# Attention with inserted projection work: the second half of v in 6 and 5 steps a tile, and the insertions as a fixed list

## The chip, the cores and the metric

The kernel runs on one core of one Trainium2 chip. The metric is the device time of one execution in microseconds (us), as the median of several runs.

## The reference

Two layers, each an attention block followed by a Fourier mixing block, on x of 2048 rows (S) and 640 columns (D), in float32.

```python
def _A_ref(x, wqkv, wo):             # H = 32 heads, Dh = 20
    qkv = (x @ wqkv).reshape(B, S, 3, H, Dh).transpose(2, 0, 3, 1, 4)
    q, k, v = qkv[0], qkv[1], qkv[2]
    scores = einsum("bhqd,bhkd->bhqk", q, k) * Dh ** -0.5
    o = einsum("bhqk,bhkd->bhqd", softmax(scores), v)
    return o.transpose(0, 2, 1, 3).reshape(B, S, D) @ wo

x = A_x                              # twice:
x = x + _A_ref(_layernorm(x), A_wqkv, A_wo)
x = x + _B_ref(_layernorm(x), ...)   # Fourier mixing by DFT matrices
```

## The kernel before

**Phases of a layer.** A prologue normalizes and transposes x, makes the first chunk of q and of k (128 columns each, that is six heads and a bit) and the first half of v for all 16 row tiles. Then comes the attention sweep, which is most of a layer's time. The rest of the projection (the other chunks of q and k, and the second half of v) is inserted into the sweep. After it come the output projection and the Fourier block.

**The sweep.** `Attention.steps` is a list of 512 steps (g, qb, kc): 8 groups g of 4 heads, 4 query blocks qb of 512 rows, 16 key tiles kc of 128 rows. Below, step n is the place in this list; 16 steps are one q block, 64 one group. A step has
- two calls of `scores` (two heads each): two matmuls into one of three `psc` tiles in PSUM (L613), then one exponential on ScalarE over 128x1024 numbers (L616);
- one call of `values`: four matmuls, one a head, that add e x v to the accumulator `acc` (L624; the profile has each of them as two records). There is one `acc` bank. At kc = 15 `finish` follows: VectorE transposes `acc` out (L631), divides by the sum, transposes back, splits the result, and POOL writes it to DRAM. `values` of kc = 0 of the next block can begin when L631 has read the bank.

**The inserted work.** `Qkv.work` is a generator. Each `next` on it emits some matmuls: a block of a chunk of q or k (15 matmuls `pqk` of 128x512 for one of four column blocks tb, in pieces of 8 and 7 or three times 5), or a tile of the second half of v (15 matmuls `pv` of 128x320 in one piece, then a copy on VectorE, L314). Both use the one PSUM bank `fill`. After a block `keep` splits it on VectorE and POOL writes it to DRAM; some steps later a function `after` adds a small matmul `pn` and its maximum, and after a chunk's last block splits the next chunk's weights and fetches those after them on SP's queue. The chunks come in the order of `order` (i = 0 to 7); in the code before, the 16 tiles of v stand between chunks 3 and 4.

**The order of instructions** is written out by hand (the tile framework runs in manual schedule). A string fixes it for some steps: `s` is one call of `scores` (half a step), `v` one of `values`, `f` the next piece of inserted work, `n` the function owed after a block. The two strings of the sweep (`plan`):

```python
if n % 4 == 1 and n + (4 if whole else 8) < s.THIN and (whole or s.blocks % 2 == 0):
    return "sssfsssvvssvv" if whole else "sssfsssvvssvvsssfssvvsssnvv"
```

The first (4 steps) inserts a tile of v, the second (8 steps) one block of q or k. They begin at step 1: 16 blocks (steps 1 to 128), 16 tiles of v (129 to 192), 5 blocks (193 to 232). I call the second the dense string. From step 236 (`THIN`) on, the thin part, steps alternate "ss v", and `fill` inserts one piece of five matmuls where n % 16 is 2, 7 or 12; the step with a piece has no `v`, and two steps later there are two. A block thus takes 16 steps, and 11 blocks last until step 412. From step 448 on other strings (`tail`) insert the output projection.

In the thin part and in all strings, work for `compare` (checks of the DFT matrices, which run on VectorE and load by POOL's queue) goes along at a pace set by n alone.

`begin` makes sure, with `need`, that what a group reads has been made. Before, group 4 (from step 256) needs the whole second half of v ("v") at step 240. `Attention.values` reads 32 columns of a tile of v at 21 columns a head, so the last head of group 3 also reads columns that belong to the second half; their products are not used.

Of the kernel before, what the change touches and what calls it, by code (L numbers as in the profile page):

```python
# [6 lines left out]
F32R = mybir.dt.float32r  # L7
# [35 lines left out]
def mha_fnet_kernel(ctx, tc, x_in, wqk, wv, wo, seq, hid, nat_seq, nat_hid, out):  # L43
# [102 lines left out]
    class Qkv:  # L146
# [199 lines left out]
        def prologue(s, vals, xt, fill, att):  # L346
# [30 lines left out]
            def ones(t):  # L377
                s.v[t] = vals(f"v{t}", [H * VW + 12], F32, "v")
                G.memset(s.v[t][:, :H * VW].rearrange("p (a c) -> p a c", c=VW)[:, :, DH:], 1.0)
                G.memset(s.v[t][:, H * VW:], 1.0)  # L380

            for t in range(NT - ND):
                ones(t)
# [89 lines left out]
            s.made |= {0, ND}  # L473


        def work(s):

            order = [ND + 1, 1, ND + 2, 2, ND + 3, 3, ND + 4, 4]
            w = {0: s.w1}

            def chunk(i):
                c = order[i]
                for tb in range(NB):
                    p = bank("fill", [128, 512], "pqk")
                    for more in pieces([s.product(p, w[i], tb, dc) for dc in range(ND)], 8 if (i, tb) < (5, 1) else 5):
                        if more:
                            yield True
                    sq = s.keep(p, c, tb, True, s.fill)

                    def after():  # L490
                        s.norms(lambda *a: bank("fill", *a), c, tb, sq)
                        s.made.add((c, tb))
                        if tb == NB - 1:
                            s.made.add(c)
                            if i + 1 < len(order):
                                w[i + 1] = s.weights(s.fill("w", [2, ND, 128], F32R, "wqk"), order[i + 1], True)
                            if i + 2 < len(order):
                                s.fetch(order[i + 2])
                    yield after

            for i in range(4):
                yield from chunk(i)
            for t in range(NT):
                p = bank("fill", [128, HD], "pv")
                for more in pieces([s.value(p, t, dc) for dc in range(ND)], 15):
                    if more:
                        yield True
                s.own(p, t, 1, True)
                yield None
            s.made.add("v")  # L510
            for i in range(4, 8):
                yield from chunk(i)

            s.silent = True
            r = s.bounds()
            ok = const.tile([128, 1], F32, name="ok", bufs=2)
            V.tensor_scalar(ok[:H], r[:H, 2:3], (GUARD / SCALE) ** 2, None, op0=OP.is_le)

            def after():
                p = bank("fill", [1, 1], "pok")  # L520
                PE.matmul(p, ok[:H], one[:H], start=True, stop=True)
                V.tensor_scalar(s.flag, p, float(H), None, op0=OP.is_equal)
            yield after
# [23 lines left out]


    class Attention:
        THIN = 236  # L550

        def __init__(s, qkv, L):
            s.a = qkv
            s.k, s.q, s.e = {}, {}, {}
# [93 lines left out]
        def sweep(s, shift, begin, fill=lambda n: None, plan=None, block=None, compare=lambda n: None):  # L648
            done = calm = n = 0

            def opened(n):
                g, qb, kc = s.steps[n]
                begin(n, g, qb, kc)
                last = qb == NB - 1
                if kc == (7 if last else 10 if g in LATE else 4) and not (last and g == H // 4 - 1):
                    s.qload(*((g, qb + 1) if not last else (g + 1, 0)), shift)
                if last and g + 1 < H // 4:
                    for f, j in {1: [(0, 0)], 9: [(0, 1)], 11: [(1, 0)]}.get(kc, []):
                        s.kload(g + 1, f, j)
                if qb == 0 and kc == 0 and g:  # L660
                    s.kload(g, 1, 1)

            while n < len(s.steps):
                opened(n)
                order = plan and plan(n)
                if order:

                    while done < n - 1:
                        s.values(done)
                        done += 1  # L670
                    t = 2 * n
                    for c in order:
                        if c == "s":
                            m, j = divmod(t, 2)
                            if not j and m > n:
                                opened(m)
                            s.scores(m, j)
                            if j:
                                compare(m)
                            t += 1  # L680
                        elif c == "v":
                            s.values(done)
                            done += 1
                        else:
                            (block if c == "f" else fill)(t // 2)
                    n = t // 2
                    continue
                s.scores(n, 0)
                s.scores(n, 1)
                more, owed = fill(n) and n >= 2 and n + 1 < len(s.steps), n - 1 - done  # L690
                compare(n)
                n += 1
                if plan and n <= s.THIN:
                    count = owed + 1
                elif more and owed < 3:
                    calm = n + 1
                    continue
                else:
                    count = min(owed, 1)
                    if owed > 1 and (done + 1) % NT and n > calm:  # L700
                        calm = n + 1
                        count = 2
                for _ in range(count):
                    s.values(done)
                    done += 1
            for n in range(done, len(s.steps)):
                s.values(n)

        def run(s, done, project, check):
# [8 lines left out]
                           8: "sssfssvssvsvssvssvssvssvv"}[steps]  # L718
                n += steps

            def due(n):
                return s.blocks < 58 or s.blocks >= 91 or (n - 1) % NT in (2, 7, 12)

            def block(n):
                if not s.work:
                    project.parts.pop(0)()
                    return
                try:
                    f = next(work)
                    s.blocks += 1  # L730
                    s.more = f is True
                    s.after = (n + (2 if n < s.THIN else 4), f) if f and not s.more else None
                    s.rest = s.after[0] + 2 if s.after else n
                except StopIteration:
                    s.work = False
                    tasks.extend(done())

            def fill(n):
                if s.after:
                    if n >= s.after[0]:  # L740
                        f, s.after = s.after[1], None
                        f()
                elif s.work and n >= max(s.rest, s.THIN) and due(n + 1):
                    block(n)
                    s.rest = max(s.rest, n + 2)
                    return s.work and not s.a.silent

            def plan(n):
                if n in tail:
                    return tail[n]  # L750
                if s.blocks >= 58 or s.after:
                    return
                whole = 32 <= s.blocks < 48
                if n % 4 == 1 and n + (4 if whole else 8) < s.THIN and (whole or s.blocks % 2 == 0):
                    return "sssfsssvvssvv" if whole else "sssfsssvvssvvsssfssvvsssnvv"

            def compare(n):

# [18 lines left out]

            def begin(n, g, qb, kc):


                if qb == NB - 1 and g + 1 < H // 4:
                    when, to = 0, g + 1
                    c0, c1 = to * 80 // 128, ((to + 1) * 80 - 1) // 128
                    keys = [c0, (c1, 0) if to in LATE else c1, ND + c0, ND + c1] + (["v"] if to >= 4 else [])
                else:
                    when, to, keys = 5, g, [(((g + 1) * 80 - 1) // 128, qb + 1)]
                if to != g or g in LATE and qb < NB - 1:
                    if kc == when:
                        need(n, *keys)
                        s.shift = s.a.bound(to, s.room)  # L790
                    if kc - when in (0, 3, 5):
                        next(s.shift)

                if tasks and n % 2 == 0 and n >= 16 and n % 64 < 54:
                    tasks.pop(0)()
                for f in project.early.get(n, []):
                    f()
# [955 lines left out]
```

## Time and profile before

| | |
|---|---|
| median of 3 runs | 2439.93 us (2438.36, 2442.01, 2439.93) |
| profiled execution, its own time | 2440.27 us |
| its span, first to last instruction | 2438.5 us |
| TensorE's granted clock | 0.998 of full |
| busy: matmuls (PE), weight loads (PEld) | 2408.8, 1154.0 us |
| busy: ScalarE (ACT), VectorE (DVE), POOL | 2098.3, 1011.4, 555.9 us |
| exponentials (L616) | 2048, busy 1917.2 us |
| matmuls of values (L624), of scores (L613) | busy 1030.6 and 743.7 us |
| inserted and prologue matmuls `pqk`, `pv` (L106) | busy 320.5 and 151.7 us |

The sweep of layer 0 lasts from about 82 to 1094 us of the span, that of layer 1 from 1293 to 2307 us. A row of a group names line, engine, operation, output<-inputs, shapes, count, then busy time, mean ns of one, and the idle time of the engine just before it with what ended it. Rows of a timeline give start, length, engine, line, operation; rows of like instructions that follow each other are merged. Ends of matmuls are modelled, so their starts are the better measure.

### The profile page before, as it was taken

Reading aid. Unit: us, or ns where it says so; the run is one execution under the profiler, and the core shown is the slowest. Engines: PE = TensorE matmul, PEld = TensorE weight load, DVE = VectorE, ACT = ScalarE, POOL = GpSimd, SP = SyncE. Lnnn points to the kernel's source line nnn. Section 1 sums busy time; section 2 is a strip of 40 time slices with the busy share of each in tenths; the row PEclk is TensorE's granted clock in tenths of the full one; section 3 lists DMA queues with packets and bytes.
Section 4 is the critical chain, followed back from the end, with each engine's and each line's share of the span. In section 5 each row is a group of like instructions: output and inputs, shape, how many; then the busy total and the mean of one; then the engine's idle time right before and its main releaser. Section 6 shows DMA issues by size and latency. Waiting matters only on the chain. (4 is left out here: it accounts for less than half of the span.)

```text
span 2438.5 us, 43843 instructions
## 1 busy us (share of the span) xinstructions
PE 2408.8 (99%) x16200; PEld 1154.0 (47%) x16200; DVE 1011.4 (41%) x2328; ACT 2098.3 (86%) x2402; POOL 555.9 (23%) x1080
## 2 busy tenths in 40 slices
PE   9999999999999999999999999999999999999998
PEld 7544445543333333349785444454433333333496
DVE  7333332334333343427763444332433333334175
ACT  5799988899999999995357999988999999999852
POOL 3122221021221212115341212211111212123143
PEclk9999999999999999999999999999999999999999
DMA  6334341223232325419663232322231322152295
GB/s 214 129 128 128 114 150 54 63 66 119 87 97 85 106 70 166 118 51 317 231 221 114 97 118 86 117 63 78 77 108 57 96 58 80 52 156 79 72 312 208
DMA packets 136702, 289.01 MB, mean 119 GB/s; under 512 B 31628, under 2 KB 56108, under 8 KB 136480
## 3 DMA queue, kind: packets, MB, share of 16 engines
q1 hardware_dynamic: 93408, 171.07, 21.6%
q0 software_dynamic: 43072, 115.06, 14.8%
q8 instruction: 130, 2.13, 0.4%
q14 instruction: 92, 0.75, 0.1%
HBM read 187.38 MB, written 92.70 MB: 115 GB/s over the span
## 5 line engine op out<-in xcount | busy, mean ns | idle before, releaser
L616 ACT ACTIVATE e<-psc 128x1024 f32<-128x1024 f32 x2048 | 1917.2, 1060 | 109.1 <-PE psc L613 98.4
L624 PE MATMUL acc<-e,v 128*32 128x512 f32 x8192 | 1030.6, 600 | 0.4 <-DVE of L631 0.4
L613 PE MATMUL psc<-stq,stk 62*128 62x512 f32 x4096 | 743.7, 445 | 3.7 <-ACT e L616 2.2
L613 PEld LDWEIGHTS psc<-stq,stk 62*128 62x128 f32 x4096 | 334.1, 184 | 700.1 <-ACT e L616 547.0
L624 PEld LDWEIGHTS acc<-e,v 128*32 128x32 f32 x8192 | 210.2, 108 | 412.3 <-issue 380.4
L106 PE MATMUL pqk<-xt,wqk 128*128 128x512 f32 x1200 | 320.5, 407 | 3.2 <-ACT xt L93 2.0
L645 POOL DMA_DIRECT2D o<-oh x256 | 131.5, 522 | 784.1 <-DVE oh L640 736.5
L91 DVE CAST hl<-pqk 128x512 fp32r<-128x512 f32 x64 | 44.3, 692 | 589.1 <-PE pqk L106 589.1
L106 PEld LDWEIGHTS pqk<-xt,wqk 128*128 128x128 f32 x1200 | 213.1, 188 | 88.2 <-issue 38.7
L106 PE MATMUL pv<-wv,xt 128*128 128x320 f32 x960 | 151.7, 313 | 0.0
L106 PEld LDWEIGHTS pv<-wv,xt 128*128 128x128 f32 x960 | 141.0, 188 | 13.5 <-issue 10.2
L631 DVE STREAM_TRANSPOSE of<-acc 128x512 f32<-128x512 f32 x64 | 45.8, 715 | 207.1 <-PE acc L624 207.1
L645 POOL DMA_DIRECT2D o<-ot x256 | 128.2, 509 | 1.8 <-DVE xr L1118 0.6
L275 POOL DMA_DIRECT2D scrk<-hl x40 | 28.0, 699 | 378.5 <-DVE hl L94 268.0
L275 POOL DMA_DIRECT2D scrq<-hl x40 | 28.5, 711 | 353.8 <-DVE hl L94 293.4
L99 PE MATMUL py<-wo,o 128*128 128x320 f32 x320 | 101.2, 316 | 3.3 <-DVE xr L1118 3.3
L914 DVE TENSOR_REDUCE far<-cq 128x1 f32<-128x512 f32 (+5 forms) x169 | 98.5, 584 | 5.7
L101 PE MATMUL py<-wo,o 128*128 128x320 f32 x320 | 98.8, 309 | 0.0
L100 PE MATMUL py<-wo,o 128*128 128x320 f32 x320 | 98.7, 308 | 0.0
L918 DVE TENSOR_TENSOR cq<-cq 128x512 f32<-128x512 f32 (+4 forms) x166 | 96.4, 581 | 1.3 <-DMA cq<-in_nat_seq_dram 1.3
L314 DVE COPY v<-pv 128x320 f32<-128x320 f32 x32 | 15.7, 490 | 161.8 <-PE pv L106 161.8
L99 PEld LDWEIGHTS py<-wo,o 128*128 128x128 f32 x320 | 60.0, 188 | 10.4 <-issue 6.1
(219 smaller groups left out, 1722.7 us busy)
## 6 DMA issues: line engine op xcount, KB each, us to landing
cq<-in_nat_seq_dram POOLq DMA_DIRECT2D x64, 512.0 KB, 5.4
scrq<-hl POOLq DMA_DIRECT2D x40, 512.0 KB, 3.5
scrk<-hl POOLq DMA_DIRECT2D x40, 512.0 KB, 3.2
stq<-scrq SPq DMA_DIRECT2D x256, 80.0 KB
stk<-scrk SPq DMA_DIRECT2D x128, 160.0 KB
chl<-matrix SPq DMA_DIRECT2D x32, 512.0 KB
o<-o SPq DMA_DIRECT2D x32, 384.0 KB
stq<-scrq SPq DMA_DIRECT2D x256, 40.0 KB
```

What stands on the lines that cost most here:

```text
L99: PE.matmul(out_ap, ah, bh, start=start, stop=False)
L100: PE.matmul(out_ap, ah, bl, start=False, stop=False)
L101: PE.matmul(out_ap, al, bh, start=False, stop=stop)
L106: yield lambda i=i, j=j, k=k: PE.matmul(out_ap, a[i], b[j], start=dc == 0 and k == 0, stop=dc == ND - 1 and k == 2)
L275: G.dma_start(s.scr["qk"[k]][c * 128:(c + 1) * 128, :, tb * 512:(tb + 1) * 512], hl.bitcast(F32))
L613: PE.matmul(p[:, i], s.k[g, kc // 8, j][r, kc % 8 * 128:(kc % 8 + 1) * 128], s.q[g, qb, j][r], start=True, stop=True)
L616: A.activation(e, p, AF.Exp, scale=SCALE)
L624: PE.matmul(s.acc[32 * j:32 * j + 32], s.a.v[kc][:, v0:v0 + 32], s.e[n, j // 2][:, j % 2], start=kc == 0, stop=kc == NT - 1, skip_group_ch ...
L631: V.transpose(t0.rearrange("p b c -> p (b c)"), s.acc)
L645: G.dma_start(s.o[k, h * DH:(h + 1) * DH, qb * 512:(qb + 1) * 512], hl[k][32 * j:32 * j + DH])
L914: V.tensor_reduce(to, x, op=OP.max, axis=AX.X, apply_absolute_value=True)
L918: V.tensor_tensor(y, x, y, op=op)
```

## The change

The insertions are a fixed list `PLAN` now, with a kind of string for each entry: chunks 0 to 4 and the first block of chunk 5 dense (21 blocks, steps 1 to 168), then 8 tiles of v in strings of 6 steps ("six", 169 to 216), two dense blocks (217 to 232), 8 tiles of v in strings of 5 steps ("five", 233 to 272), one block in a string of 10 steps ("loose", 273 to 282). From step 283 on the thin part inserts the last 8 blocks, one piece each where n % 16 is 1, 6 or 12. In all, three blocks of q and k move from the thin part into strings, and the tiles of v get 88 steps instead of 64. `need` asks for each tile of v by itself, at steps 256 to 271. Since the second half of v is no longer complete when group 3 begins (step 192), a memset on POOL sets the 20 columns behind the first half of each tile to zero.

```diff
+                G.memset(s.v[t][:, H // 2 * VW:H // 2 * VW + DH], 0.0)
...
+        PLAN = ([("dense", i, tb) for i in range(5) for tb in range(NB)] + [("dense", 5, 0)]
+                + [("six", None, t) for t in range(8)] + [("dense", 5, tb) for tb in (1, 2)]
+                + [("five", None, t) for t in range(8, NT)] + [("loose", 5, 3)]
+                + [(None, i, tb) for i in (6, 7) for tb in range(NB)])
...
-            for i in range(4):
-                yield from chunk(i)
-            for t in range(NT):
-                p = bank("fill", [128, HD], "pv")
-                for more in pieces([s.value(p, t, dc) for dc in range(ND)], 15):
-                    if more:
-                        yield True
+            def value(t):
+                p = bank("fill", [128, HD], "pv")
+                for dc in range(ND):
+                    for f in s.value(p, t, dc):
+                        f()
                 s.own(p, t, 1, True)
+                s.made.add(("v", t))
                 yield None
-            s.made.add("v")
-            for i in range(4, 8):
-                yield from chunk(i)
+
+            for kind, i, n in s.plan:
+                yield from value(n) if i is None else block(i, n, 5 if kind is None else 8)
...
-                if plan and n <= s.THIN:
+                if plan and not s.thin:
                     count = owed + 1
...
-            def due(n):
-                return s.blocks < 58 or s.blocks >= 91 or (n - 1) % NT in (2, 7, 12)
+            strings = {"dense": "sssfsssvvssvvsssfssvvsssnvv", "loose": "ssfsssvvsssvvsssfsssvvsssvvsssnvv",
+                       "six": "sssfsssvvssvssvssvv", "five": "sssfsssvvssvssvv"}
+            todo, s.thin = list(s.a.PLAN), False
...
-                    s.after = (n + (2 if n < s.THIN else 4), f) if f and not s.more else None
+                    if not s.more and todo:
+                        todo.pop(0)
+                    s.after = (n + (4 if s.thin else 2), f) if f and not s.more else None
...
-                elif s.work and n >= max(s.rest, s.THIN) and due(n + 1):
+                elif s.work and s.thin and n >= s.rest and (not todo or n % NT in (1, 6, 12)):
...
-                if s.blocks >= 58 or s.after:
-                    return
-                whole = 32 <= s.blocks < 48
-                if n % 4 == 1 and n + (4 if whole else 8) < s.THIN and (whole or s.blocks % 2 == 0):
-                    return "sssfsssvvssvv" if whole else "sssfsssvvssvvsssfssvvsssnvv"
+                if n and not s.thin and not s.after and not s.more:
+                    if todo[0][0]:
+                        return strings[todo[0][0]]
+                    s.thin = True
...
+                if (g, qb) == (H // 8, 0):
+                    need(n, ("v", kc))
...
-                    keys = [c0, (c1, 0) if to in LATE else c1, ND + c0, ND + c1] + (["v"] if to >= 4 else [])
+                    keys = [c0, (c1, 0) if to in LATE else c1, ND + c0, ND + c1]
```

In the lists below, `psc` rows are scores (four matmuls are "ss"), `acc` rows values, `pv` and `pqk` rows inserted work. TensorE, one tile of v, before:

```order
L613 MATMUL psc<-stq,stk 128x512 x6
L106 MATMUL pv<-wv,xt 128x320 x15
L613 MATMUL psc<-stq,stk 128x512 x6
L624 MATMUL acc<-e,v 32x512 x8
L613 MATMUL psc<-stq,stk 128x512 x4
L624 MATMUL acc<-e,v 32x512 x8
L613 MATMUL psc<-stq,stk 128x512 x6
```

and now, a string of six:

```order
L615 MATMUL psc<-stq,stk 128x512 x6
L106 MATMUL pv<-wv,xt 128x320 x15
L615 MATMUL psc<-stq,stk 128x512 x6
L626 MATMUL acc<-e,v 32x512 x8
L615 MATMUL psc<-stq,stk 128x512 x4
L626 MATMUL acc<-e,v 32x512 x4
L615 MATMUL psc<-stq,stk 128x512 x4
L626 MATMUL acc<-e,v 32x512 x4
L615 MATMUL psc<-stq,stk 128x512 x4
L626 MATMUL acc<-e,v 32x512 x8
L615 MATMUL psc<-stq,stk 128x512 x6
```

Two single "v" with "ss" between them now follow the first pair of "v".

TensorE at step 288, the end of a q block in the thin part (a new number of `acc` is the new block's accumulator), before:

```order
L613 MATMUL psc_6973<-stq_484,stk_480 128x512 x2
L613 MATMUL psc_6978<-stq_485,stk_481 128x512 x2
L624 MATMUL acc_6727<-e_6940,v_886 32x512 x2
L624 MATMUL acc_6727<-e_6945,v_886 32x512 x2
L613 MATMUL psc_7009<-stq_484,stk_480 128x512 x2
L613 MATMUL psc_7014<-stq_485,stk_481 128x512 x2
L106 MATMUL pqk_7019<-xt_246,wqk_6964 128x512 x3
L106 MATMUL pqk_7019<-xt_249,wqk_6964 128x512 x2
L613 MATMUL psc_7025<-stq_484,stk_480 128x512 x2
L613 MATMUL psc_7030<-stq_485,stk_481 128x512 x2
L624 MATMUL acc_7035<-e_6954,v_272 32x512 x2
L624 MATMUL acc_7035<-e_6959,v_272 32x512 x2
```

and now:

```order
L106 MATMUL pqk_6927<-xt_249,wqk_6891 128x512
L106 MATMUL pqk_6927<-xt_252,wqk_6891 128x512 x3
L106 MATMUL pqk_6927<-xt_255,wqk_6891 128x512
L615 MATMUL psc_7012<-stq_495,stk_491 128x512 x2
L615 MATMUL psc_7017<-stq_496,stk_492 128x512 x2
L626 MATMUL acc_6739<-e_6970,v_901 32x512 x2
L626 MATMUL acc_6739<-e_6975,v_901 32x512 x2
L615 MATMUL psc_7046<-stq_495,stk_491 128x512 x2
L615 MATMUL psc_7051<-stq_496,stk_492 128x512 x2
L626 MATMUL acc_7056<-e_6984,v_272 32x512 x2
L626 MATMUL acc_7056<-e_6989,v_272 32x512 x2
L626 MATMUL acc_7056<-e_6998,v_276 32x512 x2
```

Before, "ss", a piece and "ss" stand between the last value matmul of the old block and the first of the new; now the piece stands ahead of the last, and "ss" alone is between.

TensorE at step 256, where group 4 begins inside a string of five, now:

```order
L626 MATMUL acc_6054<-e_6288,v_897 32x512 x2
L626 MATMUL acc_6054<-e_6310,v_897 32x512 x2
L615 MATMUL psc_6350<-stq_495,stk_491 128x512 x2
L615 MATMUL psc_6355<-stq_496,stk_492 128x512 x2
L626 MATMUL acc_6054<-e_6315,v_901 32x512 x2
L626 MATMUL acc_6054<-e_6320,v_901 32x512 x2
L626 MATMUL acc_6384<-e_6339,v_272 32x512 x2
L626 MATMUL acc_6384<-e_6344,v_272 32x512 x2
L615 MATMUL psc_6389<-stq_495,stk_491 128x512 x2
L615 MATMUL psc_6394<-stq_496,stk_492 128x512 x2
```

The last "v" of the old block and the first of the new are one pair, with nothing between; before, a piece and two "ss" stood there as at step 288.

More of the change, by code (lines that the diff above doesn't have):

```diff
@@ L473, in prologue, with block @@
             s.made |= {0, ND}
+        PLAN = ([("dense", i, tb) for i in range(5) for tb in range(NB)] + [("dense", 5, 0)]
+                + [("six", None, t) for t in range(8)] + [("dense", 5, tb) for tb in (1, 2)]
+                + [("five", None, t) for t in range(8, NT)] + [("loose", 5, 3)]
+                + [(None, i, tb) for i in (6, 7) for tb in range(NB)])
         def work(s):
-            order = [ND + 1, 1, ND + 2, 2, ND + 3, 3, ND + 4, 4]
-            w = {0: s.w1}
-            def chunk(i):
+            s.plan = s.PLAN
+            order, w = [ND + 1, 1, ND + 2, 2, ND + 3, 3, ND + 4, 4], {0: s.w1}
+            def block(i, tb, size):
@@ L482, in chunk @@
                 c = order[i]
-                for tb in range(NB):
-                    p = bank("fill", [128, 512], "pqk")
-                    for more in pieces([s.product(p, w[i], tb, dc) for dc in range(ND)], 8 if (i, tb) < (5, 1) else 5):
-                        if more:
-                            yield True
[L488 to L499, printed above, removed]
@@ L501, in work @@
-            for i in range(4):
-                yield from chunk(i)
-            for t in range(NT):
-                p = bank("fill", [128, HD], "pv")
-                for more in pieces([s.value(p, t, dc) for dc in range(ND)], 15):
+                p = bank("fill", [128, 512], "pqk")
+                for more in pieces([s.product(p, w[i], tb, dc) for dc in range(ND)], size):
                     if more:
                         yield True
+                sq = s.keep(p, c, tb, True, s.fill)
@@ new lines, in after @@
+                def after():
+                    s.norms(lambda *a: bank("fill", *a), c, tb, sq)
+                    s.made.add((c, tb))
+                    if tb == NB - 1:
+                        s.made.add(c)
+                        if i + 1 < len(order):
+                            w[i + 1] = s.weights(s.fill("w", [2, ND, 128], F32R, "wqk"), order[i + 1], True)
+                        if i + 2 < len(order):
+                            s.fetch(order[i + 2])
+                yield after
@@ L549, in mha_fnet_kernel @@
     class Attention:
-        THIN = 236
         def __init__(s, qkv, L):
@@ L729, in block @@
                     f = next(work)
-                    s.blocks += 1
                     s.more = f is True
-                    s.after = (n + (2 if n < s.THIN else 4), f) if f and not s.more else None
+                    if not s.more and todo:
+                        todo.pop(0)
+                    s.after = (n + (4 if s.thin else 2), f) if f and not s.more else None
                     s.rest = s.after[0] + 2 if s.after else n
```

## Prediction

> **What bounds the kernel now.** I read the page first (share by engine, costliest groups), then the windows of the exponentials (L616), cut where a kind of string begins, then the timeline of TensorE, ScalarE and VectorE inside single strings.
>
> ```profile
> PE 2408.8 (99%) x16200; PEld 1154.0 (47%) x16200; DVE 1011.4 (41%) x2328; ACT 2098.3 (86%) x2402; POOL 555.9 (23%) x1080
> L616 ACT ACTIVATE e<-psc 128x1024 f32<-128x1024 f32 x2048 | 1917.2, 1060 | 109.1 <-PE psc L613 98.4
> ```
>
> TensorE is busy nearly all the time, and where the exponentials idle, they wait for its scores. Two exponentials are one step, so a stretch between counted exponentials is a number of steps. Columns below: stretch, its length, ScalarE's busy time in L616 (count, including those that straddle an edge).
>
> ```profile
> 83.74:348.12 264.38, 240.95 (x258) 1.00 0.38 124
> 348.12:485.17 137.05, 120.84 (x128) 1.00 0.23 73
> 485.17:567.70 82.53, 75.27 (x81) 1.00 0.30 97
> 567.70:661.89 94.19, 93.23 (x101) 1.00 0.28 88
> 663.70:906.93 243.23, 239.75 (x258) 1.00 0.29 89
> 916.48:943.60 27.12, 27.12 (x31) 1.00 0.39 118
> 1294.45:1559.80 265.35, 240.72 (x258) 1.00 0.34 107
> 1559.80:1696.85 137.05, 120.84 (x128) 1.00 0.24 74
> 1696.85:1779.58 82.73, 75.25 (x80) 1.00 0.28 88
> 1779.58:1873.80 94.22, 93.24 (x100) 1.00 0.26 77
> ```
>
> In layer 0 these are: steps 1 to 128 (16 dense strings), 129 to 192 (16 tiles of v), 193 to 232 (5 dense), 233 to 282 (thin, 50 steps), 284 to 411 (thin, 128 steps), 417 to 431 (nothing inserted, 15 steps); then the first four again in layer 1. So:
> - a dense string (8 steps) takes (264.38 + 82.53) / 21 = 16.52 us in layer 0, (265.35 + 82.73) / 21 = 16.58 in layer 1;
> - a tile of v in 4 steps takes 137.05 / 16 = 8.566;
> - an exponential that never waits takes 27.12 / 30 = 0.904, so ScalarE alone needs 1.808 a step;
> - 16 thin steps take 243.23 / 8 = 30.40, which is 1.47 over 16 x 1.808. They hold three pieces of five matmuls, so a piece costs 0.49.
>
> Inside one tile of v, on TensorE and ScalarE:
>
> ```profile
> 356.20 0.96 PE L613 MATMUL psc<-stq,stk 62*128 62x512 f32 x6
> 357.10 2.47 PE L106 MATMUL pv<-wv,xt 128*128 128x320 f32 x15
> 359.50 0.97 PE L613 MATMUL psc<-stq,stk 62*128 62x512 f32 x6
> 360.39 1.92 PE L624 MATMUL acc<-e,v 128*32 128x512 f32 x16
> 362.25 0.73 PE L613 MATMUL psc<-stq,stk 62*128 62x512 f32 x4
> 362.91 1.92 PE L624 MATMUL acc<-e,v 128*32 128x512 f32 x16
> 364.76 0.98 PE L613 MATMUL psc<-stq,stk 62*128 62x512 f32 x6
> 365.67 0.56 PE L106 MATMUL pv<-wv,xt 128*128 128x320 f32 x2
> 360.10 4.71 ACT L616 ACTIVATE e<-psc 128x1024 f32<-128x1024 f32 x5 [0.44 <-PE psc L613]
> 365.37 1.03 ACT L616 ACTIVATE e<-psc 128x1024 f32<-128x1024 f32 x1 [0.56 <-PE psc L613]
> ```
>
> From start to start, "sss" takes 0.90, the tile's 15 matmuls 2.40, "vv" 1.86, "ss" 0.66. Each row begins before the one ahead of it ends, so TensorE has no hole, and ScalarE idles twice for it. The inserted strings run at TensorE's pace, and the question is how many microseconds of TensorE the new strings hold, not how much slack ScalarE has.
>
> One rule speaks against this reading of the first row. The Trainium skill (Trainium Kernel Development and Optimization, Performance Expectations) calls matmul busy time a bad metric, since matmuls are pipelined, and points to the weight loads' busy share, here 47%. By that, ScalarE would set the pace of the new strings (the last rival); the releasers and the starts above, not the 99%, are why I keep TensorE.
>
> **The change, part by part, for one layer.**
>
> *The longer v strings.* "six" is the old string with "ss v" put in twice, "five" with it put in once. The price is in the rows where single steps alternate already:
>
> ```profile
> 987.05 0.73 PE L613 MATMUL psc<-stq,stk 62*128 62x512 f32 x4
> 987.72 1.07 PE L624 MATMUL acc<-e,v 128*32 128x512 f32 x8
> 988.71 0.73 PE L613 MATMUL psc<-stq,stk 62*128 62x512 f32 x4
> ```
>
> "ss" 0.67, a single "v" 0.99, together 1.66. So six = 8.566 + 2 x 1.66 = 11.89 and five = 10.23 us. ScalarE would need 12 x 0.904 = 10.85 and 9.04, less in both, so TensorE stays the bound. A step added this way (1.66) is cheaper than a thin step with its share of pieces (30.40 / 16 = 1.90), but dearer than a step of the old tile (the 8.566 less 2.40, over 4: 1.54), because "vv" and "sss" cost less than their parts. The Trainium skill (TensorEngine Tiling (Array Packing), Tiling Modes) says that changing the tiling mode drains TensorE; scores, values and inserted work use three shapes of the array (62*128, 128*32, 128*128 in the rows). Without any such price a step would cost the added "s" and "v" alone (2 x 0.24 + 0.87 = 1.35), and the sum below would be 8 x 2 x 0.31 + 8 x 0.31 = 7.4 us a layer lower, about 2427; the 0.67 and 0.99 of the rows already hold it, so I go by them.
>
> *Two dense strings and a loose one in place of 9 thin pieces.* Two dense are 33.04. The loose one is a dense string with two more "sss" and one more "vv" but one "ss" less: 16.52 + 1.80 + 1.86 - 0.66 = 19.52; ScalarE needs 18.08.
>
> *Sum to step 283*, layer 0: 23 x 16.52 + 8 x 11.89 + 8 x 10.23 + 19.52 = 379.96 + 95.12 + 81.84 + 19.52 = 576.44, against 264.38 + 137.05 + 82.53 + 94.19 = 578.15 before: -1.7. Layer 1: 577.8 against 579.35: -1.5.
>
> *The end of a q block.* There is one accumulator bank. After the v of kc 15, VectorE transposes it out (L631), and the v of kc 0 waits for that. The order before puts "sss f sss" or "ss f ss" between the two everywhere up to step 400, the new one only "ss" at steps 176, 208, 240 and 288, 304, ... 400, and nothing at 256. The price, where "ss" alone already stands between:
>
> ```profile
> 976.11 1.06 PE L624 MATMUL acc<-e,v 128*32 128x512 f32 x8
> 977.11 0.88 PE L613 MATMUL psc<-stq,stk 62*128 62x512 f32 x4
> 977.25 0.72 DVE L631 STREAM_TRANSPOSE of<-acc 128x512 f32<-128x512 f32 x1 [0.42 <-PE acc L624]
> 978.02 1.06 PE L624 MATMUL acc<-e,v 128*32 128x512 f32 x8
> ```
>
> From "v" to "v" 1.91 us, where 1.66 is the undisturbed pair: 0.25 lost. With nothing between, the second "v" could start 0.93 after the first (half of 1.86), so 0.98 is lost. In the strings that is 3 x 0.25 + 0.98 = 1.73, all of it on TensorE, which has no hole to take it: queued behind the waiting "v" are the next scores, and ScalarE waits for those. That takes back the gain: 0.0 in layer 0, +0.2 in layer 1.
>
> *The thin part from step 283.* Its pieces move from steps 2, 7, 12 of a block to 1, 6, 12. There are 24 instead of 25 from there on (-0.49), and the first finds ScalarE two exponentials ahead after four "s" in a row, so I take its cost off too (bounds 0 and -0.49). A piece at 1 puts the v of kc 15 behind it, just where TensorE is already late:
>
> ```profile
> 613.98 1.42 PE L106 MATMUL pqk<-xt,wqk 128*128 128x512 f32 x5
> 615.33 0.73 PE L613 MATMUL psc<-stq,stk 62*128 62x512 f32 x4
> 615.99 1.06 PE L624 MATMUL acc<-e,v 128*32 128x512 f32 x8
> 616.99 0.73 PE L613 MATMUL psc<-stq,stk 62*128 62x512 f32 x4
> 617.64 1.92 PE L624 MATMUL acc<-e,v 128*32 128x512 f32 x16
> 619.50 0.73 PE L613 MATMUL psc<-stq,stk 62*128 62x512 f32 x4
> ```
>
> After a piece TensorE runs without a hole; in the new order the wait falls between the second "ss" and the "vv", and delays the scores that ScalarE is short of. 8 boundaries x 0.25 = +2.0; bounds 0 (absorbed) and 0.98 each. Net +1.0.
>
> *What costs nothing.* The 16 memsets (a layer) of 128x20:
>
> ```profile
> L380 POOL MEMSET v<- x32: 111/115/122, 9.9 to 1274.5; 128x12 f32 x32
> 1226.36 0.76 POOL L275 DMA_DIRECT2D scrq<-hl  x1 [3.17 <-DVE hl L274]
> 359.61 0.49 DVE L314 COPY v<-pv 128x320 f32<-128x320 f32 x1 [6.65 <-PE pv L106]
> ```
>
> About 0.12 each, eleven in a row, 1.3 us, ahead of an idle 3.17 on POOL; without that cover 1.3 a layer. The copies of a tile (0.49) end at 360.10, before the "vv" at 360.39, so even where the new order reads that tile's columns at once (strings at 233 and 253) 0.29 is left. The moved dense blocks take with them four VectorE operations and one POOL write each, and the fetch of raw weights on SP's queue; all of them come earlier than before (the last block of this kind ends near step 283 instead of 288), so nobody waits longer. The new wait for single tiles of v (steps 256 to 271) finds each made at least two steps before.
>
> **Sum.** (0.0 + 1.0) + (0.2 + 1.0) = +2.2 us on the profiled execution, whose own time is 2440.27 (its span, 2438.5, plus 1.8 around it): 2442.5. That execution lies 0.34 above the median 2439.93, so against the median 2442.1; I say 2442. This is +0.09%. The runs before spread from 2438.36 to 2442.01, so a difference under 0.2%, 4.9 us (2435.0 to 2444.8), can't be told from none.
>
> **The rivals.**
> - *The waits at block ends are absorbed* (faster): ScalarE or the pipeline already lags as much there, all 24 short boundaries cost nothing, and 2 x (1.73 + 2.0) = 7.5 comes off: 2434.6. For it: in the thin part ScalarE works through 98.6% of the time (239.75 of 243.23). Against it: there is no hole in TensorE after a piece.
> - *VectorE comes late to the transposes* (slower): if a comparison's operation (L918 or L914, some 0.69 us) is running when the v of kc 15 ends, the transpose starts about 0.6 later, and the order now has no cover for it. At 5 of 24 boundaries it decides (2445.1); at half of them 2442 + 12 x 0.6 = 2449. For it: VectorE is 41% busy. Against it: in the row at 977.25 it had idled 0.42 before the transpose.
> - *ScalarE sets the pace of the new strings* (faster): 8 x (11.89 - 10.85) + 8 x (10.23 - 9.04) = 17.8 a layer off, 2406. Against it stand the two idle times in each tile of four steps, and the 1.66 from TensorE alone. It is what the rule of the Trainium skill on matmul busy time (Trainium Kernel Development and Optimization, Performance Expectations) would lead to.
>
> **How the numbers follow.** Forecast 0.66, absorbed 0.13, VectorE late 0.18, ScalarE's pace 0.03. The forecast's own range is 2438 (thin waits absorbed) to 2446 (two more adjacent-like waits a layer); about 0.03 of it lies above 2444.8. So faster 0.15, same 0.65, slower 0.20. The range 2435 to 2449 leaves out the last rival, half of the first, and half of the second.
>
> **What would show it.** Right: strings of about 11.9 and 10.2 us; TensorE without holes in them except 0.25 before the first "v" of a block and about 1 us at step 256; thin blocks of 30.6 to 30.7 instead of 30.40; nearly the same time at step 283. Wrong: thin blocks still at 30.40 (absorbed); waits of the first "v" above 0.6 (VectorE late); strings near 10.9 and 9.1 (ScalarE's pace).

## The result, and the profile after

The changed kernel takes 2444.53 us (median of 13 runs, 2440.89 to 2448.88), against 2438.43 for the kernel before in 13 runs beside them (2434.20 to 2442.01). The ratio is 1.0027 [1.0018, 1.0035], so +6.1 us. The forecast was 2442, that is +2.2 us: the time lies inside its range, but the change costs nearly three times what I worked out, and the middle of the interval is past the 0.2% that I had called telling. One execution of all those in this document, of the kernel before with the memsets, took 4453.44 us, nearly twice the others of its kernel; it is left out of the ratio and of the difference given for that run.

The profiled execution hides this. Its own time, 2440.89, is the lowest of the 13, and its span is only 0.5 us longer than before's. So the comparison below goes by the sweeps, cut at counted exponentials.

The page of the kernel after: busy share by engine, and the two groups that changed; then, from the page of before, the group that answers to the last one. The last two fields are idle time just before the group and what ended it.

```profile
PE 2404.0 (99%) x16200; PEld 1157.5 (47%) x16200; DVE 1012.9 (42%) x2328; ACT 2099.5 (86%) x2402; POOL 557.9 (23%) x1112
L618 ACT ACTIVATE e<-psc 128x1024 f32<-128x1024 f32 x2048 | 1918.1, 1066 | 113.1 <-PE psc L615 106.1
L626 PE MATMUL acc<-e,v 128*32 128x512 f32 x8192 | 1027.8, 600 | 7.7 <-DVE of L633 7.7
```

```profile
L624 PE MATMUL acc<-e,v 128*32 128x512 f32 x8192 | 1030.6, 600 | 0.4 <-DVE of L631 0.4
```

TensorE is still busy 99% of the span, with 4.8 us less of it. What is new is one releaser: the value matmuls now wait 7.7 us for VectorE's transpose of the accumulator, where they had waited 0.4. The exponentials idle 4.0 us more in all (113.1 for 109.1), and the part that waits for scores is 106.1 for 98.4.

The windows of the exponentials (L618) in the kernel after, cut where the kinds of strings begin; the columns are those of the windows in the prediction. The first ten rows are layer 0: steps 1 to 128, 129 to 168 (5 dense), 169 to 192 (4 "six"), 193 to 216 (4 "six"), 217 to 224 (one dense), 225 to 272 (one dense, 8 "five"), 273 to 282 (loose), 283 to 410, 411 to 447, 448 to 453 (the first string of `tail`). The last four are layer 1: 1 to 128, 129 to 282, 283 to 410, 448 to 453.

```profile
82.90:347.06 264.16, 240.93 (x258) 1.00 0.38 125
347.06:429.50 82.44, 75.15 (x81) 1.00 0.34 113
429.50:477.53 48.03, 44.89 (x48) 1.00 0.23 74
477.53:525.35 47.82, 44.88 (x49) 1.00 0.19 55
525.35:541.82 16.47, 15.19 (x17) 1.00 0.19 51
541.82:641.47 99.65, 90.17 (x96) 1.00 0.25 80
641.47:661.74 20.27, 18.76 (x20) 1.00 0.34 104
661.74:906.90 245.16, 240.47 (x256) 1.00 0.29 89
906.90:975.09 68.19, 67.98 (x76) 1.00 0.50 156
975.09:987.06 11.97, 11.21 (x13) 1.00 0.27 80
1291.95:1556.14 264.19, 240.91 (x258) 1.00 0.33 108
1556.14:1870.80 314.66, 289.04 (x308) 1.00 0.26 80
1870.80:2116.02 245.22, 240.49 (x257) 1.00 0.24 72
2184.20:2196.30 12.10, 11.21 (x12) 1.00 0.26 77
```

The same steps in the kernel before, layer 0: 129 to 232, 233 to 282, 283 to 410, 411 to 447, 448 to 453.

```profile
348.12:567.70 219.58, 196.12 (x209) 1.00 0.26 82
567.70:661.89 94.19, 93.23 (x101) 1.00 0.28 88
661.89:905.12 243.23, 239.75 (x257) 1.00 0.29 89
905.12:973.67 68.55, 68.16 (x76) 1.00 0.47 150
973.67:984.95 11.28, 11.10 (x12) 1.00 0.50 138
```

In layer 0, steps 129 to 282 took 313.77 before and take 314.68 now, +0.9; the thin part to 410 takes 245.16 for 243.23, +1.9; then -0.4 (one piece fewer), and the string at step 448 takes 11.97 for 11.28, +0.7. From step 454 on nothing differs (+0.03). That is +3.2. Layer 1 adds +3.1 by the same cut, together **+6.3 us, which is the measured +6.1**. Left out of this sum are steps 1 to 128 and what lies outside the two sweeps: the change does not touch TensorE's work there, and the lengths vary from one execution to the next (last section).

### The profile page after: what moved, and what is told of

The parts are those of the page before. It is cut to its first block, busy times and chain, and to the rows that moved or that the text cites. A ratio compares the mean times of both kernels' runs of the same rounds, so it can differ in the third digit from the quotient of the medians.

```text
span 2439.0 us, 43878 instructions
## 1 busy us (share of the span) xinstructions
PE 2404.0 (99%) x16200; PEld 1157.5 (47%) x16200; DVE 1012.9 (42%) x2328; ACT 2099.5 (86%) x2402; POOL 557.9 (23%) x1112
## 5 line engine op out<-in xcount | busy, mean ns | idle before, releaser
L618 ACT ACTIVATE e<-psc 128x1024 f32<-128x1024 f32 x2048 | 1918.1, 1066 | 113.1 <-PE psc L615 106.1
```

The source lines that it names most:

```text
L618: A.activation(e, p, AF.Exp, scale=SCALE)
```

## The experiments

My theory after the result: all of the loss is TensorE time, in four places, each of them visible in the trace. (1) The new strings end q blocks with "ss" or nothing between the accumulator's last "v" and the next block's first. (2) So do the thin blocks, since their pieces stand at 1, 6, 12. (3) With 24 thin pieces at those places the inserted work is over 6 steps sooner (the last piece comes at step 406 instead of 412), and a task of VectorE lands ahead of the transpose at step 448. (4) The loose string is dearer than TensorE's sum. The main rivals: the strings themselves (their length, the memsets, more pressure on ScalarE) cost the time, or all block ends are absorbed.

A table of all runs comes first. The trace columns are the sums over both layers against before, by counted exponentials as above; "measured" is the difference of medians to runs of the kernel before on the same chip.

| kernel | steps 129-282 | 283-410 | 411-447 | 448-453 | trace, sum | measured | ratio |
|---|---|---|---|---|---|---|---|
| after | +1.6 | +3.9 | -0.7 | +1.5 | +6.3 | +6.1 | 1.0027 [1.0018, 1.0035] |
| after, thin pieces at 2, 7, 12 | +1.8 | -0.8 | 0.0 | 0.0 | +1.0 | +2.5 | 1.0008 [0.9999, 1.0017] |
| after, end of the work held back | +1.9 | +4.0 | -0.7 | 0.0 | +5.2 | +6.4 | 1.0026 [1.0016, 1.0036] |
| strings realigned, thin 1, 6, 12 | -1.9 | +3.9 | -0.7 | +1.5 | +2.8 | +4.6 | 1.0019 [1.0010, 1.0028] |
| strings realigned, thin 2, 7, 12 | -1.4 | -1.0 | 0.0 | 0.0 | -2.4 | -2.5 | 0.9987 [0.9978, 0.9996] |
| strings realigned, thin 3, 8, 13 | -1.5 | +4.8 | +0.5 | 0.0 | +3.9 | +6.6 | 1.0028 [1.0017, 1.0039] |
| before, plus the memsets | 0.0 | +0.1 | 0.0 | 0.0 | +0.2 | -0.5 | 1.0000 [0.9992, 1.0009] |
| before, thin pieces at 1, 6, 12 | +2.1 | +4.0 | -0.7 | +1.5 | +6.9 | +7.9 | 1.0034 [1.0021, 1.0047] |

**The thin pieces put back** where they stood in the kernel before, all else as after:

```diff
-                elif s.work and s.thin and n >= s.rest and (not todo or n % NT in (1, 6, 12)):
+                elif s.work and s.thin and n >= s.rest and (not todo or n % NT in (2, 7, 12)):
```

> The changed kernel with the thin pieces back at 2, 7, 12 of a block; everything else as changed. Theory A (the loss is in what stands between the last v of a q block and the first of the next): 'ss f ss' stands there again from step 288 to 400, so a thin block falls from 30.65 to 30.40 us (-2.0 a layer). The inserted work also ends at step 416 to 418 as in the kernel before, so VectorE's weight work moves back and the first tail string (step 448) falls from 12.0 to 11.3 (-0.7 a layer). Together -5.4 against the changed kernel: about +1 us against before (within 0.1%). Theory B (the loss is in the longer v strings themselves, in the memsets, or outside the sweep): thin blocks may fall, but the median stays near +6 us.

2439.88 against 2437.42: not told apart from before; 0.19 of the 0.27% are gone. Seven of its eight thin blocks take 30.38 to 30.44, as in the kernel before (30.37 to 30.43); the other, from step 299, has one piece fewer and takes 30.00, which is the -0.8 of the table. The string at step 448 takes 11.29 and 11.30. What remains, +1.8 in the trace, is in the strings.

**The end of the work held back** to step 418, nothing else moved:

```diff
-                elif s.work and s.thin and n >= s.rest and (not todo or n % NT in (1, 6, 12)):
+                elif s.work and s.thin and n >= s.rest and (n >= 418 if not todo else n % NT in (1, 6, 12)):
```

> The changed kernel with pieces at 1, 6, 12, but what follows the last block (the guard's check, then the projection's weights) held back until step 418, as in the kernel before. Theory A: only the first tail string changes, from 12.0 to 11.3 us (-0.7 a layer, since the split of wo no longer runs on VectorE just ahead of the transpose at step 448); thin blocks stay at 30.65; the whole is about 1.4 us under the changed kernel, +4.7 against before. Rival: the string at 448 is long for another reason (the shift by one step of the v behind the pieces), and stays at 12.0; no change.

First the two timelines that made me try it. VectorE and TensorE at step 448 in the kernel after:

```profile
978.17 0.48 DVE L91 CAST wo<-woraw 128x640 fp32r<-128x640 f32 x1
978.69 0.82 DVE L94 TENSOR_TENSOR wo<-woraw,wo 128x640 fp32r<-128x640 f32 x1
979.43 0.71 DVE L633 STREAM_TRANSPOSE of<-acc 128x512 f32<-128x512 f32 x1
977.53 1.06 PE L626 MATMUL acc<-e,v 128*32 128x512 f32 x8
980.20 1.06 PE L626 MATMUL acc<-e,v 128*32 128x512 f32 x8 [0.79 <-DVE of L633]
```

The split of a row block of `wo` (a cast and a subtraction) runs on VectorE just as the block's last "v" ends at about 978.6; the transpose follows it back to back, 0.8 late, and the next "v" starts 2.67 after the last instead of 1.91. In the kernel before (VectorE, same place; the transpose is the row at 977.25 in the prediction) the two stand well ahead and well behind it:

```profile
964.89 0.48 DVE L91 CAST wo<-woraw 128x640 fp32r<-128x640 f32 x1
...
981.04 0.49 DVE L91 CAST wo<-woraw 128x640 fp32r<-128x640 f32 x1
```

With the end held back (VectorE and TensorE of that run):

```profile
968.20 0.48 DVE L91 CAST wo<-woraw 128x640 fp32r<-128x640 f32 x1
980.22 0.72 DVE L633 STREAM_TRANSPOSE of<-acc 128x512 f32<-128x512 f32 x1 [0.42 <-PE acc L626]
980.99 1.06 PE L626 MATMUL acc<-e,v 128*32 128x512 f32 x8
```

The split is back where it was, VectorE idles 0.42 before the transpose as in the kernel before, and the string takes 11.30 in both layers. So place (3) is shown, worth 1.5 us over two layers. The time of the whole kernel does not show it: 1.0026 against 1.0027, with intervals of about 0.1% to each side.

**The strings realigned.** An order in which no block end falls into a string without cover: the first 22 blocks dense, then the 16 tiles as six, five, five in turn (16 steps, one q block), then the loose block, and the last dense one.

```diff
-        PLAN = ([("dense", i, tb) for i in range(5) for tb in range(NB)] + [("dense", 5, 0)]
-                + [("six", None, t) for t in range(8)] + [("dense", 5, tb) for tb in (1, 2)]
-                + [("five", None, t) for t in range(8, NT)] + [("loose", 5, 3)]
+        PLAN = ([("dense", i, tb) for i in range(5) for tb in range(NB)] + [("dense", 5, 0), ("dense", 5, 1)]
+                + [("five" if t % 3 else "six", None, t) for t in range(NT)] + [("loose", 5, 2), ("dense", 5, 3)]
```

> The changed kernel with its strings in another order: 22 dense ones, then tiles of v as six, five, five (16 steps, so each q block ends with a string), loose, dense; thin pieces at 1, 6, 12 as changed. No wait of the first v is left before step 288. Theory A: every six takes 11.88, every five 10.21; to step 283 about 577.3 us from step 1 instead of 578.8 (-1.5 a layer); thin blocks 30.65 and the string at 448 stay. About -3 us against the changed kernel, +3 against before. Theory B (the tensor time of the longer strings is what costs, not the waits at block ends): no gain in the strings, +6 against before.

The windows of the exponentials in this run, layer 0: steps 129 to 232, 233 to 282.

```profile
348.66:560.76 212.10, 195.21 (x208) 1.00 0.27 87
560.76:661.60 100.84, 93.81 (x101) 1.00 0.26 81
```

Together 312.94, against 314.68 after and 313.77 before, so 1.74 us less. The two orders are not quite alike: the new one has six strings of six and ten of five, and two steps more of the thin part. By its own strings (11.91 and 10.21, and 3.63 for the two steps) that alone would be 2 x 10.21 + 3.63 - 2 x 11.91 = +0.2, and its loose string takes 0.1 more. So the new order is worth some 2.0 a layer. In the kernel after, the four strings in which the bare ends fall are longer than the shortest of their kind by 0.25 (step 176), 0.27 (208), 0.26 (240) and 1.05 (256): 1.8 together, where I had put 1.73. The other 0.2 is in strings without a bare end: three of the kernel after are 0.11 to 0.14 over the shortest (12.01 twice and 10.32), and one of the new order (12.02). Place (1) is shown. The whole kernel is 4.6 slower than before, since the thin part still costs its 3.9 and the string at step 448 its 1.5.

**Both together,** the realigned strings and pieces at 2, 7, 12.

> Both: the strings in the order six, five, five, and thin pieces at 2, 7, 12. Theory A: no short cover is left up to step 400; to step 283 about 577.3 us (before: 578.2), thin blocks 30.40, the string at 448 11.3: -4.2 a layer against the changed kernel, about 2 to 3 us faster than before (-0.1%), the gain that TensorE's own sum has without the waits. Theory B: about as slow as the changed kernel.

The window of steps 283 to 410 in layer 0 (those of steps 129 to 282 are as in the run before, 212.11 and 100.84) and the value matmuls' group:

```profile
660.02:902.70 242.68, 239.58 (x258) 1.00 0.28 88
L625 PE MATMUL acc<-e,v 128*32 128x512 f32 x8192 | 1027.7, 600 | 0.4 <-DVE of L632 0.4
```

2434.92 against 2437.42, ratio 0.9987 [0.9978, 0.9996]: **this version beats both kernels**, the one before by little; the interval only just leaves out 1, and part of the 2.5 us may be the granted clock (last section), but the trace sum, -2.4, is taken where that clock was 1.00. The wait for the transpose is back at 0.4 us; the idea of the change, v in longer strings, is a gain once no block end is bare. Measured it is 7.1 us faster than the realigned strings alone; the trace sums give 5.2. The two intervals of about 0.1% cover the rest, and the granted clock of these runs was higher (0.9980 in the mean, 0.9966 there).

**The memsets alone,** on the kernel before:

```diff
+                G.memset(s.v[t][:, H // 2 * VW:H // 2 * VW + DH], 0.0)
```

> The kernel before with the 16 memsets of 128x20 a layer added and nothing else. Theory A: they stand ahead of idle time on POOL and cost nothing: no change (within 0.1%), the exponentials begin where they did. Theory B (part of the +6 us lies outside the order of TensorE): up to 1.3 us a layer, +2.6 us, and later first exponentials.

Ratio 1.0000 [0.9992, 1.0009]. They cost nothing that can be measured.

**The kernel before with thin pieces at 1, 6, 12,** none of the new strings:

```diff
-                return s.blocks < 58 or s.blocks >= 91 or (n - 1) % NT in (2, 7, 12)
+                return s.blocks < 58 or s.blocks >= 91 or (n - 1) % NT in (1, 6, 12)
```

> The kernel before with its thin pieces at 1, 6, 12 of a block and nothing else: no new strings, no memsets. Theory A: 'ss' alone stands between the last v and the first at 11 block ends (240 to 400), 0.25 each, so thin blocks of 30.65 instead of 30.40 from step 284 on, +2.7 a layer; the work also ends some steps earlier, which puts VectorE's weight work ahead of the transpose at step 448 (first tail string 12.0 instead of 11.3, +0.7). About +6 us in all: the changed kernel's loss without the changed strings. Theory B (the strings cost it): less than +2.

Its windows in layer 0, steps 283 to 410 and 448 to 453:

```profile
665.62:910.87 245.25, 240.53 (x257) 1.00 0.29 90
979.06:991.04 11.98, 11.21 (x12) 1.00 0.27 81
```

Both lengths are those of the kernel after to 0.1 us, and the kernel is 7.9 us slower than before: moving two of three small pieces by a single step loses as much as the whole change did. That the new strings alone cause the loss is out.

**Pieces at 3, 8, 13,** on the version that beats both:

```diff
-                elif s.work and s.thin and n >= s.rest and (not todo or n % NT in (2, 7, 12)):
+                elif s.work and s.thin and n >= s.rest and (not todo or n % NT in (3, 8, 13)):
```

> The strings in the order six, five, five, with thin pieces at 3, 8, 13 of a block. The v of kc 15 and that of kc 0 then have only 'ss' between them, as with 1, 6, 12, but the wait falls six steps after the last piece, not right behind one. Theory A: TensorE has caught up there and would wait for ScalarE anyway, so the wait is absorbed: thin blocks of 30.40, the whole within 0.1% of the same kernel with 2, 7, 12 (the work ends some steps later, so the string at 448 may move). Rival (a wait of the first v costs its 0.25 wherever it falls): thin blocks of 30.65, +4 us against it.

A piece at 3 comes behind the first "v" of the new block, so the block ends are bare again, but no piece stands just ahead of the last "v"; I had looked for the short wait to be absorbed. It was half right. In layer 0, three of the four blocks up to step 346 take 30.45 to 30.48, only 0.1 over the 30.34 to 30.39 of the version above (the fourth has one piece fewer in both, 29.99); those from 363 on take 30.65 to 30.69. And at step 352 in layer 0 this happened (VectorE, then TensorE):

```profile
794.49 0.68 DVE L284 TENSOR_REDUCE top<-pn 32x1 f32<-32x512 f32 x1 [2.63 <-PE pn L283]
795.09 0.47 DVE L91 CAST wqk<-wraw 128x640 fp32r<-128x640 f32 x1
795.60 0.83 DVE L94 TENSOR_TENSOR wqk<-wraw,wqk 128x640 fp32r<-128x640 f32 x1
796.34 0.68 DVE L921 TENSOR_TENSOR cq<-cq 128x512 f32<-128x512 f32 x1
797.06 0.69 DVE L917 TENSOR_REDUCE far<-cq 128x1 f32<-128x512 f32 x1
797.66 0.70 DVE L632 STREAM_TRANSPOSE of<-acc 128x512 f32<-128x512 f32 x1
798.42 0.64 PE L625 MATMUL acc<-e,v 128*32 128x512 f32 x4 [2.45 <-DVE of L632]
```

The block's last "v" ends at 795.3; VectorE has the maximum of `pn`, the split of the next weights and a comparison in front of the transpose, and TensorE stands still for 2.45 us. Layer 1 has the same place 0.96 late, and step 416 there 0.62. So a bare block end costs as little as 0.1 to 0.25 only while VectorE is free; the rival "VectorE late" of the prediction is real, and the cover of a piece is what keeps it from being felt. In the kernel before the transposes at steps 288 and 352 of layer 0 start 1.77 and 1.76 after the last "v" instead of 1.13, and from "v" to "v" it is 3.67 and 3.68 there, as at step 400 (3.67), where the transpose was not late. Why the short wait is absorbed early and not from step 363 on I did not separate by a run. (The order has a `pn` matmul ahead of the block end in the later blocks.)

## Why the prediction was right and wrong

**Right: the price of the strings.** Eight "six" take 48.03 + 47.82 with two bare block ends; less 0.25 for each of these that is 11.92 (forecast 11.89). "Five": 99.65, less a dense 16.47, less 0.25 and 1.04 for two bare ends, leaves 81.89 / 8 = 10.24 (forecast 10.23). The dense ones take 82.44 / 5 = 16.49 (16.52). TensorE, not ScalarE, sets their pace: the rival drawn from the rule of the Trainium skill on matmul busy time (Trainium Kernel Development and Optimization, Performance Expectations) put the kernel 36 us faster, with strings of 10.85 and 9.04, and the strings show none of that.

**Right: the wait at a bare block end.** TensorE in the kernel after, at step 288 (first three rows) and at step 256 (the others):

```profile
674.81 1.06 PE L626 MATMUL acc<-e,v 128*32 128x512 f32 x8
675.81 0.73 PE L615 MATMUL psc<-stq,stk 62*128 62x512 f32 x4
676.74 1.92 PE L626 MATMUL acc<-e,v 128*32 128x512 f32 x16 [0.21 <-DVE of L633]
...
607.32 1.07 PE L626 MATMUL acc<-e,v 128*32 128x512 f32 x8
609.22 1.07 PE L626 MATMUL acc<-e,v 128*32 128x512 f32 x8 [0.84 <-DVE of L633]
```

From "v" to "v" 1.93 and 1.90, as at the one place where before had shown it (1.91); the string around step 256 takes 11.26, 1.04 more than its neighbours (0.98 forecast). All eight thin blocks of layer 0 pay: 30.61 to 30.68, in the mean 245.16 / 8 = 30.65, in the middle of the 30.6 to 30.7 that I had named. The price holds where TensorE sets the pace. In the kernel before, "ss" alone stands at the end at step 432 too (1.90 from "v" to "v"), nothing is inserted there, and the exponentials of steps 426 to 437 go on 0.90 to 0.91 us apart: that end costs nothing.

**Wrong, three terms of the sum,** together about 2 us a layer:

- *The first thin piece at no cost* (-0.49 a layer, taken from between the bounds 0 and -0.49): not saved. Steps 283 to 410 gained their full eight waits and nothing came off (245.16 - 243.23 = 1.93, for 8 x 0.25 = 2.0), and the block with that piece takes 30.61, the next one 30.62.
- *The loose string at 19.52:* it takes 20.27. TensorE in the kernel after, inside it, with one weight load (PEld); the last row is behind the string:

```profile
644.47 1.92 PE L626 MATMUL acc<-e,v 128*32 128x512 f32 x16
646.32 1.26 PE L615 MATMUL psc<-stq,stk 62*128 62x512 f32 x6
647.08 0.19 PEld L615 LDWEIGHTS psc<-stq,stk 62*128 62x128 f32 x2 [0.46 <-ACT e L618]
647.51 1.92 PE L626 MATMUL acc<-e,v 128*32 128x512 f32 x16
649.37 0.97 PE L615 MATMUL psc<-stq,stk 62*128 62x512 f32 x6
650.26 1.88 PE L106 MATMUL pqk<-xt,wqk 128*128 128x512 f32 x7
662.82 0.50 PE L615 MATMUL psc<-stq,stk 62*128 62x512 f32 x2 [0.71 <-ACT e L618]
```

  "sss" at 646.32 lasts 1.19 to the next start, where the one at 649.37 lasts 0.89, and 1.23 and 1.20 at two places further on. Between two "sss" with only "vv" between them lie 0.90 + 1.86 = 2.76 us of TensorE for three exponentials of 0.904, and the three `psc` tiles let TensorE run no further ahead: wherever ScalarE has fallen behind, the next "sss" waits for it, 0.3 each time; at 647.08 it is an exponential that releases the weights of its third call. These waits hardly appear in the page's idle time of the scores. The 1.4 us by which scores wait longer for exponentials there (3.6, before 2.2) are the last row, 0.71 in each layer, ahead of the first thin piece. I had compared ScalarE's 18.08 with the whole string and not place by place. That the three tiles are the reason is read from the rows, not tried by a run.
- *The earlier end of the inserted work at no cost:* +0.7 to +0.8 a layer at step 448, by the second experiment. I had seen to it that the moved blocks' own tasks come early enough, but not what comes after the last of them: the tasks that wait for the work to be over shift too.

With these three the sum is 2442.1 + 2 x (0.5 + 0.75 + 0.75) = 2446.1 on the median that the forecast stood on, 2439.93; with the measured +6.1 that median gives 2446.0. Smaller terms are off too: the piece that is gone gave 0.37 and 0.34 instead of 0.49, the bare ends in the strings took 1.8 instead of 1.73, and layer 1's dense strings were 16.49 and not 16.58.

**The chances.** "Same" at 0.65 was too high: each term that I had set at the cheap end of its bounds came out dearer, and none erred the other way. On the median of the forecast the measured difference gives 2446.0, the upper end of the forecast's own range (2438 to 2446). That the time lies well inside the whole range is in part luck: the range to 2449 had been widened for VectorE coming late. That did happen, but once a layer, at a block end that was bare before too, and by a task shifted in time rather than by a comparison; that is 1.5 of the 4 us that the sum lacked, and the other 2.5 come from two terms that no bound of the range was drawn from.

## What to carry to other kernels

With a single accumulator, look at what stands between the last use of one block and the first of the next at every block end of a new order, also where only steps modulo the block are renumbered: a piece of other work there (here 5 matmuls, 1.4 us) hid the hand-over, and without it each end cost some 0.25 us where TensorE set the pace, or all of VectorE's queue when that happened to be full. When work is moved, also follow the tasks that start when it is over. Price a string against the slower engine at each place between two buffers' reuse, not by its total alone.

## What the runs showed that I had not expected

- Steps 1 to 128, the same strings in all kernels, take one of two lengths: 264.2 to 264.4 or 265.3 to 265.8 us. After's profiled execution had the short one twice (264.16, 264.19), before's one of each (264.38, 265.35). A sum over the sweep that contains them can be off by 2.9 us. In layer 0 the granted clock makes the difference. Four executions have the long one there (265.7), all of it in step 2, and in these TensorE's granted clock is 0.50 at that place (0.52 in one); in the other five it is 1.00. The first inserted piece, at 84 to 87 us of the span, in the run with the end held back and in the kernel after (the column behind the count is the clock):

```profile
84.00:87.00 3.00, 3.00 (x8) 0.50 0.43 135
84.00:87.00 3.00, 3.00 (x22) 1.00 0.43 127
```

  In layer 1 most of the long one is some 0.28 us more at each of steps 23, 55, 87 and 119, with the clock at 1.00; why is open.
- The stretch between the two sweeps took 193.8 to 198.4 us in nine executions: 198.4 in before's profile and 193.8 in after's. That is why after's span was only 0.5 us longer with sweeps that are 4.9 longer. Again the clock divides them: in the three longest (198.4, 196.4, 195.6) it was 0.91 in the mean from 1180 to 1200 us, in the six others (193.8 to 194.4) it was 1.00 throughout. One profiled execution can't be set against another by its span where 0.2% matter.
- The same shows in the times of all runs. Among runs of one kernel, 0.001 less of mean granted clock goes with about 1.8 us more (an estimate, a straight line through all runs with a clock on record). So where the "measured" column lies above the trace sum, part of it can be the clock: the runs with pieces at 3, 8, 13 had 0.9964 in the mean, those of the kernel before beside them 0.9972. Whether an order of work changes how often the clock falls is not shown.
